# The tiles of x start at 64 modulo 256 bytes in place of 0

## The chip, the cores and the metric

The kernel runs on one core of a Trainium2 chip. The metric is the device time of one execution in microseconds. PE is TensorE (PEld its weight loads), DVE is VectorE, ACT is ScalarE, POOL is GpSimd, SP is SyncE, which here only starts DMAs.

## The reference

A windowed attention (768 positions, 8 heads of 64, a batch of 4) is followed by a feed-forward layer with a rational activation. Cut to what matters:

```python
scores = scale * np.matmul(q, k.transpose(0, 1, 3, 2))
scores = np.where(keep, scores + bias, -1e9)        # a local window of 96 and 8 global keys
a = softmax(scores)
x = np.matmul(a, v)                                 # -> (3072 tokens, 512)
h = x @ w_in                                        # (512, 2048)
P = a[0] + a[1] * h + a[2] * h**2 + a[3] * h**3
Q = 1.0 + np.abs(b[0]) * np.abs(h) + np.abs(b[1]) * h**2
out = (P / (Q + 1e-06)) @ w_out                     # (2048, 512)
```

## The kernel before

The 3072 tokens are worked in 12 chunks of 256. Each chunk has 8 attention units (a pair of heads for 128 tokens each) and 8 feed-forward units f (256 of the 2048 columns of w_in each). A program of tokens (LEAD), a loop over t with priorities (PRI) and a last list (TAIL) set the order of the instructions on every engine; PE and SP follow the order of the code.

The products of the feed-forward layer keep float32's precision with three float32r matmuls each: a high and a low part of one operand against a high and a low part of the other (high by high, low by high, high by low). For chunk 0 alone x stays one float32 tile, x0, and line 332 multiplies it in float32; the names below are those of chunks 1 to 11.

- `st_x` (line 737) takes the attention's output of a chunk out of PSUM. ACT writes the high part into the tile xh (line 753), DVE the low part, xl (line 763, in `st_xl`). Each is 128 partitions by 4 x 256 numbers, 4096 bytes of a partition. There are two buffers of each, used in turn by the chunks.
- `st_ffn1` (line 322) computes h = x @ w_in for one unit in two halves y. Line 340 issues 12 matmuls for each half: 4 tiles of 128 rows, and for each the products high weight by xh, high weight by xl, low weight by xh. The **stationary** operand, which a LDWEIGHTS loads, is a block of 128 x 128 of the weights; the **moving** operand is 256 columns of xh or xl. A unit is 24 such matmuls in a row.
- The activation runs on ACT, DVE and POOL and leaves g, high and low.
- `st_ffn2` (line 426) multiplies by w_out: line 442 issues 12 matmuls for a unit. Here g is stationary and 512 columns of w_out (high or low) move. `st_last2` (line 445) does the same for the last unit, and there, at the end, on half the columns: line 451 has matmuls of 256 moving columns too.

Where tiles stand: pools are laid one behind the other in a partition, each tile behind the one made first before it. A small tile `gap` of 24 numbers (line 218) stands at the end of the constants, so that all that follows starts at 64 modulo 256. Start addresses in the built program, in bytes of a partition:

| tile | start | modulo 256 | used by |
|---|---|---|---|
| win_h, high weights of w_in | 2368 | 64 | line 340, stationary |
| wout_h, high weights of w_out | 18752 | 64 | lines 442 and 451, moving |
| h tiles, the rest of the high weights | 52544 and on, each 4096 | 64 | lines 340 (stationary), 442 (moving) |
| w..l, low weights | 85312 and on, each 2048 | 64 | lines 340 (stationary), 442 (moving) |
| pad0 | 183616 | 64 | nobody |
| xh, two buffers | 183808, 187904 | 0 | line 340, moving |
| xl, two buffers | 192000, 196096 | 0 | line 340, moving |
| pad1 | 200192 | 0 | nobody |
| sp, the six buffers of the activation, g | 200256 and on | 64 | g: lines 442 and 451, stationary |

The blocks that a matmul takes out of these tiles lie at multiples of 512 bytes from their start, so the remainder modulo 256 is the same for each of them. Line 340 thus has its moving operand at 0 and its stationary one at 64; lines 442 and 451 have both at 64.

The two pads are tiles that `pad` (line 494) makes and POOL sets to zero, when chunk 1's first tiles of x are made (line 743 ff.).

Of the kernel before, what the change touches and what calls it, by code (L numbers as in the profile page):

```python
# [9 lines left out]
F32 = mybir.dt.float32  # L10
# [7 lines left out]
P = 128  # L18
# [124 lines left out]
def tile_kernel(ctx: ExitStack, tc: tile.TileContext, q, k, v, n_global, n_local,  # L143
                w_in, w_out, ca, cb, out):
    nc = tc.nc
# [16 lines left out]
    pl = SimpleNamespace(tmps=TMPS, gbufs=GBUFS, split=False)  # L162
# [5 lines left out]
    def unit(u):  # L168
        c, j = divmod(u, UPC)
        t, p = divmod(j, NPAIR)  # L170
        b, i = divmod(2 * c + t, NT)
        return c, t, p, b, i
# [51 lines left out]
    def staged(dt, shape, name):  # L224
        return stage.tile([P, *shape], dt, tag="s", name=name, bufs=8)
# [265 lines left out]
    pTs = {}  # L491
    ops = {}

    def pad(pool, n, name):
        nc.gpsimd.memset(pool.tile([P, n], F32, tag=name, name=name, bufs=1), 0.0)

    def blocks_of(x, i):
        return x if i else x[..., 0, :]

# [209 lines left out]
    def run_of(u):  # L709
        return 4 if u >= PAIRS else 2  # L710
# [26 lines left out]
    def st_x(u0):  # L737
        n, m = run_of(u0), u0 // 2
        c, t, p, b, i = unit(u0)
        if c not in xT and c == 0:  # L740
            xT[c] = staged(F32, (NCT, TOK), "x0")
        elif c not in xT:
            if c == 1:
                pad(pl.att, 48, "pad0")
            xT[c] = (pl.att.tile([P, NCT, TOK], FR, tag="xh", name=f"xh{c}"),
                     pl.att.tile([P, NCT, TOK], FR, tag="xl", name=f"xl{c}"))
            if c == 1:
                pad(pl.att, 16, "pad1")
        cs = slice(t * P, (t + 1) * P)
        if c == 0:  # L750
            nc.scalar.copy(out=xT[c][:, p:p + n, cs], in_=ops.pop(m))
            return
        nc.scalar.copy(out=xT[c][0][:, p:p + n, cs], in_=ops[m])
# [13 lines left out]
    def windowed():  # L767
# [4 lines left out]
        for x in range(2):  # L772
# [14 lines left out]
        parts = dict(L=lambda u: st_load(u, True), V=load_v, sp=st_split, sr=st_gather, qT=st_qkT, qE=st_qkE, kG=st_kG,  # L787
                     s=st_score, kg=st_kg, t=st_max, x=st_soft, r=st_total, n=st_norm, T=st_pT, tw=st_spread, P=st_pTE, zw=st_scatter, vp=load_vp, o=st_pv,
                     vg=st_vg, y=st_x, z=st_xl, W=w_load, a=w_scale, b=w_floor, c=w_sign, d=w_bits, h=w_high, l=w_low,
                     f1=st_ffn1, e1=st_ew1, e2=st_poly, eq=st_sum, e3=st_ew3, e4=st_ew4, gh=st_high, gl=st_low, f2=st_ffn2,  # L790
                     BL=st_blocks, BZ=st_zero, H=st_hold, O=st_out, D=st_send, F=st_last2)
# [289 lines left out]
```

## Time and profile before

| | |
|---|---|
| median of 3 runs | 695.6 us (694.66 to 695.7) |
| profiled execution | 694.39 us, its span 692.6 us |
| PE busy | 666.9 us, 96% of the span |
| DVE, ACT, POOL busy | 536.0, 531.6, 365.4 us |
| line 340 | 2112 matmuls, 31% of the chain that ended last |
| line 442 | 1032 matmuls, 31% of that chain |

The profile lists each instruction with its start and how long it took. Matmuls overlap, and their ends are modelled: a matmul of line 340 is listed with some 280 ns, though the next one starts some 115 ns later. What one costs is therefore read from start to start, or from the chain of work that ended last, which lists matmuls that follow each other as one piece with its length. "PEclk" is the share of TensorE's clock that was granted, 1.00 being 2.4 GHz.

### The profile page before, as it was taken

To read this page: it belongs to the slowest core of one execution; us is meant where nothing else is said; L and a number is where in the kernel's file an instruction comes from. 1 tells how busy PE (TensorE), PEld (TensorE's weight loads), DVE (VectorE), ACT (ScalarE), POOL (GpSimd) and SP (SyncE) were. 2 spreads that over 40 slices of the span, in tenths; PEclk is the share of its full clock that TensorE was granted. 3 is DMA by queue.
4 is the path that set the end of the run, shared out by engine and by line. 5 is a ranking of instruction groups with operands and counts; after the bars stand their busy time and mean duration, and the time that the engine had idled before them with its cause. 6 is when DMAs were issued, how large, how long until landed. Compare 5 with 4: busy or idle time off the path is not lost.

```text
span 692.6 us, 17121 instructions
## 1 busy us (share of the span) xinstructions
PE 666.9 (96%) x6167; PEld 572.6 (83%) x6167; DVE 536.0 (77%) x1319; ACT 531.6 (77%) x1174; POOL 365.4 (53%) x487
## 2 busy tenths in 40 slices
PE   5799999999999999999999999999999999999995
PEld 4577768768788898888889889888889889898994
DVE  5899999897987777777787777777777777765664
ACT  6899999876677877777786876876887876866773
POOL 2475545676446456456556546545555545543441
PEclk9999999999999999999999999999999999999998
DMA  7874646413576757655557657655457555320001
GB/s 189 272 207 101 208 119 188 121 46 87 146 183 164 184 127 179 158 138 142 139 132 183 167 129 180 166 127 152 132 139 188 151 150 150 101 85 1 31 2 36
DMA packets 161215, 95.22 MB, mean 137 GB/s; under 512 B 100064, under 2 KB 141152, under 8 KB 161120
## 3 DMA queue, kind: packets, MB, share of 16 engines
q1 hardware_dynamic: 161120, 94.02, 52.0%
q8 instruction: 51, 0.84, 0.6%
q14 instruction: 44, 0.36, 0.2%
HBM read 66.39 MB, written 27.59 MB: 136 GB/s over the span
## 4 chain that ended last, share of the span: by engine, by line
PE 74%; ACT 11%; DVE 7%; DMA 2%; issue 2%; POOL 1%; SPq 1%; DVEq 0%; POOLq 0%; ACTq 0%
PE h L340 31%; PE acc L442 31%; PE o L724 5%; PE s L601 4%; ACT pr L645 2%; ACT r L271 1%; PE acc L438 1%; DMA r<-in_moe_w_in_dram 1%; ACT qzero L564 1%; DVE fu L404 1%; DVE q L403 1%; PE h L332 1%; DVE fu L402 1%; ACT fs L397 1%; DVE pr L636 1%
## 5 line engine op out<-in xcount | busy, mean ns | idle before, releaser
L386 POOL TENSOR_TENSOR fa<-fa,fs 128x512 f32<-128x512 f32 (+1 forms) x86 | 110.0, 1279 | 144.2 <-ACT fs L374 143.9
L397 ACT ACTIVATE fs<-fa,coef 128x512 f32<-128x512 f32 (+1 forms) x97 | 69.8, 720 | 87.1 <-POOL fa L386 84.6
L658 POOL TENSOR_SCALAR pr<-pr,stats 128x160 f32<-128x160 f32 (+2 forms) x170 | 68.3, 421 | 128.2 <-DVE stats L652 87.0
L402 DVE SCALAR_TENSOR_TENSOR fu<-fu,coef,q 128x512 f32<-128x512 f32 (+1 forms) x97 | 71.6, 738 | 62.2 <-ACT q L398 61.8
L442 PE MATMUL acc<-wout_h,g 128*128 128x512 f32 x352 | 117.1, 393 | 2.0 <-POOL g L415 2.0
L415 POOL TENSOR_TENSOR g<-fu,g 128x512 fp32r<-128x512 f32 x84 | 108.1, 1287 | 10.1 <-ACT g L412 5.9
L442 PE MATMUL acc<-h,g 128*128 128x512 f32 x336 | 110.8, 391 | 0.1
L340 PE MATMUL h<-xh,win_h 128*128 128x256 f32 x352 | 101.3, 288 | 0.2 <-DVE fu L382 0.2
L340 PE MATMUL h<-xh,h 128*128 128x256 f32 x352 | 101.0, 287 | 0.0
L340 PE MATMUL h<-xl,win_h 128*128 128x256 f32 x352 | 98.3, 279 | 0.5 <-DVE xl L763 0.5
L340 PE MATMUL h<-xl,h 128*128 128x256 f32 x352 | 98.2, 279 | 0.0
L645 ACT ACTIVATE pr<-pr,stats 128x160 f32<-128x160 f32 (+2 forms) x192 | 82.5, 433 | 10.9 <-DVE stats L636 10.9
L372 ACT ACTIVATE fu<-h,coef 128x512 f32<-128x512 f32 x94 | 73.0, 776 | 22.9 <-PE h L340 21.8
L381 DVE TENSOR_TENSOR fu<-fu,h 128x512 f32<-128x512 f32 (+1 forms) x97 | 65.6, 677 | 31.0 <-ACT fs L374 29.6
L442 PEld LDWEIGHTS acc<-wout_h,g 128*128 128x128 f32 x352 | 65.9, 188 | 15.0 <-POOL g L415 2.8
L442 PEld LDWEIGHTS acc<-h,g 128*128 128x128 f32 x336 | 63.0, 188 | 12.5 <-POOL g L415 0.6
L382 DVE SCALAR_TENSOR_TENSOR fu<-fu,coef,h 128x512 f32<-128x512 f32 (+1 forms) x97 | 71.2, 734 | 2.7
L403 DVE SCALAR_TENSOR_TENSOR q<-fa,coef,q 128x512 f32<-128x512 f32 (+1 forms) x97 | 72.1, 743 | 0.0
L340 PEld LDWEIGHTS h<-xh,win_h 128*128 128x128 f32 x352 | 66.1, 188 | 4.4 <-issue 1.8
L340 PEld LDWEIGHTS h<-xh,h 128*128 128x128 f32 x352 | 66.1, 188 | 4.3 <-issue 2.8
L340 PEld LDWEIGHTS h<-xl,win_h 128*128 128x128 f32 x352 | 66.2, 188 | 2.1 <-DVE xl L763 0.7
L404 DVE SCALAR_TENSOR_TENSOR fu<-q,fu 128x512 f32<-128x512 f32 (+1 forms) x97 | 66.2, 682 | 2.1
(262 smaller groups left out, 1676.3 us busy)
## 6 DMA issues: line engine op xcount, KB each, us to landing
pT<-z SPq DMA_DIRECT2D x30, 512.0 KB, 4.0
z<-T SPq DMA_DIRECT2D x120, 80.0 KB, 2.3
zq<-sp SPq DMA_DIRECT2D x144, 64.0 KB, 1.8
qk<-zq SPq DMA_DIRECT2D x36, 256.0 KB, 2.8
r<-in_moe_w_in_dram SPq DMA_DIRECT2D x16, 512.0 KB, 5.1
r<-in_moe_w_out_dram SPq DMA_DIRECT2D x16, 512.0 KB, 4.0
nat<-in_q_dram SPq DMA_DIRECT2D x48, 128.0 KB, 4.2
nat<-in_k_dram SPq DMA_DIRECT2D x48, 128.0 KB, 4.0
```

The costliest lines, as they stand in the source:

```text
L340: nc.tensor.matmul(out=h_of(f, y), lhsT=w[:, fs], rhs=x[:, ct, :], start=(n == 0), stop=(n == 3 * NCT - 1))
L372: nc.scalar.activation(out=u, in_=h, func=AF.Identity, scale=a3, bias=a2)
L382: nc.vector.scalar_tensor_tensor(out=u, in0=u, scalar=a1, in1=h, op0=ALU.add, op1=ALU.mult)
L386: pace(side(f, SUM_V).tensor_tensor(out=a, in0=a, in1=s, op=ALU.add))
L397: nc.scalar.activation(out=s, in_=a, func=AF.Ln, bias=q1)
L402: nc.vector.scalar_tensor_tensor(out=u, in0=u, scalar=a0, in1=r, op0=ALU.add, op1=ALU.mult)
L403: nc.vector.scalar_tensor_tensor(out=r, in0=a, scalar=q1, in1=r, op0=ALU.add, op1=ALU.mult)
L404: nc.vector.scalar_tensor_tensor(out=u, in0=r, scalar=2.0, in1=u, op0=ALU.subtract, op1=ALU.mult, reverse0=True)
L415: pace(side(f, G_V, f == NU - 1 and ys == 1).tensor_tensor(out=gs[f][:, 1, ys], in0=ew[f]["u"][:, ys], in1=gs[f][:, 0, ys], op=ALU.subtract))
L442: nc.tensor.matmul(out=acc, lhsT=gs[f][:, z, y, ts], rhs=w, start=(start and n == 0), stop=(stop and n == 2))
L645: nc.scalar.activation(out=d, in_=d, func=AF.Exp, scale=-1.0, bias=st[:, x:x + 1], accum_out=st[:, 2 + 2 * x:3 + 2 * x])
L658: (nc.vector if u < NORMS else nc.gpsimd).tensor_scalar(out=d, in0=d, scalar1=st[:, 6 + x:7 + x], scalar2=0.0, op0=ALU.mult, op1=ALU.add)
```

## The change

The helper `pad` and its two calls go. Nothing else in the code is changed.

```diff
-    def pad(pool, n, name):
-        nc.gpsimd.memset(pool.tile([P, n], F32, tag=name, name=name, bufs=1), 0.0)
-
...
         elif c not in xT:
-            if c == 1:
-                pad(pl.att, 48, "pad0")
             xT[c] = (pl.att.tile([P, NCT, TOK], FR, tag="xh", name=f"xh{c}"),
                      pl.att.tile([P, NCT, TOK], FR, tag="xl", name=f"xl{c}"))
-            if c == 1:
-                pad(pl.att, 16, "pad1")
```

The pads were 192 and 64 bytes. Without them the built program has the buffers of xh at 183616 and 187712 and those of xl at 191808 and 195904, all 64 modulo 256. All tiles behind them stand 256 bytes lower, so their remainder is what it was; all tiles ahead of them stay. Line 340 then has both operands at 64 modulo 256, as lines 442 and 451 had before.

On PE, DVE, ACT and SP the same instructions stand in the same order. On POOL two are gone. There, before, in the attention of the first chunks (k and kG are keys, pr the probabilities of a unit, r and w parts of the weights):

```order
L658 TENSOR_SCALAR pr_701<-pr_701,stats 128x256 x2
L611 COPY k_174<-kG_65 128x8
L495 MEMSET pad_775 128x48
L495 MEMSET pad_779 128x16
L658 TENSOR_SCALAR pr_735<-pr_735,stats 128x256 x2
L273 TENSOR_SCALAR r_7_753<-r_7_753 128x512
L290 TENSOR_TENSOR w_0_0l<-w_0_0f,win_h 128x512
```

And after, at the same place on POOL (line numbers are 3 lower there, since the lines of `pad` are gone):

```order
L655 TENSOR_SCALAR pr_701<-pr_701,stats 128x256 x2
L608 COPY k_174<-kG_65 128x8
L655 TENSOR_SCALAR pr_735<-pr_735,stats 128x256 x2
L273 TENSOR_SCALAR r_7_753<-r_7_753 128x512
L290 TENSOR_TENSOR w_0_0l<-w_0_0f,win_h 128x512
```

The two MEMSETs left the row, and nothing took their place.

## Rows read from the trace of the kernel before

**Rows 1.** The page: PE's busy time, and the chain's shares by engine.
```profile
PE 666.9 (96%) x6167; PEld 572.6 (83%) x6167; DVE 536.0 (77%) x1319; ACT 531.6 (77%) x1174; POOL 365.4 (53%) x487
...
PE 74%; ACT 11%; DVE 7%; DMA 2%; issue 2%; POOL 1%; SPq 1%; DVEq 0%; POOLq 0%; ACTq 0%
```

**Rows 2.** Stretches: length, busy us of PE, PEld, DVE, ACT, POOL, PEclk, DMA.
```profile
60.00:200.00 140.00, 135.83 (x968) 105.22 (x966) 127.37 (x287) 118.05 (x265) 80.61 (x102) 1.00 0.45 126
200.00:400.00 200.00, 199.64 (x2189) 176.99 (x2190) 152.75 (x383) 152.47 (x329) 110.57 (x141) 1.00 0.63 157
400.00:600.00 200.00, 200.00 (x2132) 178.23 (x2131) 151.04 (x377) 151.51 (x324) 110.75 (x142) 1.00 0.59 148
```

**Rows 3.** The chain by time, 605 to 628 us: start us, length us, what.
```profile
605.45 2.92 PE h L340 x24
608.37 2.73 PE acc L442 x12
611.10 2.83 PE h L340 x24
613.93 2.72 PE acc L442 x12
616.65 2.83 PE h L340 x24
...
627.74 1.90 PE o L724 x32
```

**Rows 4.** Timeline of PE, a unit of line 340 behind attention: start us, us, what.
```profile
346.66 0.38 PE L340 MATMUL h<-xh,win_h 128*128 128x256 f32 x1
346.88 0.28 PE L340 MATMUL h<-xl,win_h 128*128 128x256 f32 x1
347.00 0.28 PE L340 MATMUL h<-xh,w_1l 128*128 128x256 f32 x1
...
349.38 0.28 PE L340 MATMUL h<-xh,w_1l 128*128 128x256 f32 x1
349.49 0.39 PE L442 MATMUL acc<-wout_h,g 128*128 128x512 f32 x1
349.72 0.40 PE L442 MATMUL acc<-w_2l,g 128*128 128x512 f32 x1
349.95 0.62 PE L442 MATMUL acc<-wout_h,g 128*128 128x512 f32 x2
350.41 0.39 PE L442 MATMUL acc<-w_3l,g 128*128 128x512 f32 x1
```

**Rows 5.** Timeline of PE, the next unit of line 340, behind line 442.
```profile
352.00 0.39 PE L442 MATMUL acc<-wout_h,g 128*128 128x512 f32 x1
352.22 0.28 PE L340 MATMUL h<-xh,h 128*128 128x256 f32 x1
352.34 0.28 PE L340 MATMUL h<-xl,h 128*128 128x256 f32 x1
...
355.05 0.39 PE L442 MATMUL acc<-wout_h,g 128*128 128x512 f32 x1
```

**Rows 6.** Line 340 from 346.95 to 349.35 us: count, ns min/median/max, first and last start.
```profile
L340 PE MATMUL h<-xl,win_h x8: 276/276/276, 346.9 to 349.3; 128*128 128x256 f32 x8
L340 PEld LDWEIGHTS h<-xh,w_1l x8: 187/188/188, 346.9 to 349.3; 128*128 128x128 f32 x8
```

**Rows 7.** The same of line 340 from 352.25 to 354.90 us.
```profile
L340 PE MATMUL h<-xl,h x8: 281/281/281, 352.3 to 354.8; 128*128 128x256 f32 x8
L340 PEld LDWEIGHTS h<-xh,w_2l x8: 192/192/192, 352.3 to 354.8; 128*128 128x128 f32 x8
```

**Rows 8.** Those two stretches, columns as in rows 2.
```profile
346.90:349.30 2.40, 2.40 (x23) 2.40 (x23) 2.40 (x12) 2.22 (x9) 0.67 (x1) 1.00 0.35 87
352.30:354.90 2.60, 2.60 (x24) 2.60 (x23) 1.52 (x3) 1.14 (x2) 2.60 (x3) 1.00 1.23 285
```

**Rows 9.** Timeline of PE at the end, line 451 with 256 moving columns.
```profile
684.28 0.28 PE L451 MATMUL acc<-h,g 128*128 128x256 f32 x1
684.39 0.28 PE L451 MATMUL acc<-w_15l,g 128*128 128x256 f32 x1
684.51 0.28 PE L451 MATMUL acc<-h,g 128*128 128x256 f32 x1
685.31 0.39 PE L451 MATMUL acc<-h,g 128*128 128x256 f32 x1 [0.52 <-DVE o L471]
685.53 0.28 PE L451 MATMUL acc<-w_15l,g 128*128 128x256 f32 x1
685.65 0.28 PE L451 MATMUL acc<-h,g 128*128 128x256 f32 x1
```

**Rows 10.** Timeline of POOL at the pads: start us, us, what, [idle before, releaser].
```profile
55.09 0.18 POOL L495 MEMSET pad<- 128x48 f32 x2
61.04 1.36 POOL L658 TENSOR_SCALAR pr<-pr,stats 128x256 f32<-128x256 f32 x2 [5.76 <-DVE stats L652]
```

**Rows 11.** The writers of xh and xl (as in rows 6), and a cast to a tile at 64 (as a group: busy us, mean ns).
```profile
L753 ACT CAST xh<-o x26: 373/565/582, 58.3 to 629.7; 128x512 fp32r<-128x512 f32 x18, 128x256 fp32r<-128x256 f32 x8
L763 DVE TENSOR_TENSOR xl<-o,xh x26: 404/670/683, 62.0 to 631.1; 128x512 fp32r<-128x512 f32 x18, 128x256 fp32r<-128x256 f32 x8
L286 ACT CAST win_h<-w_1f 128x512 fp32r<-128x512 f32 x4 | 2.5, 633 | 0.0
```

## The prediction

> **What bounds the kernel now.** I read the page first: PE is busy for 96% of the span and holds 74% of the chain that ended last [rows 1]. Then the busy times by stretch: from 200 to 600 us PE is busy for all but 0.4 of 400 us, while from 60 to 200 us it stands idle for 4.2 of 140 [rows 2]. Then the chain in order of time, which from about 200 us on runs through PE and repeats one pattern [rows 3]. A stretch of attention matmuls comes first, then a unit of line 340 (24 matmuls), a unit of line 442 (12), a unit of line 340, a unit of line 442. PE sets the end there, so a nanosecond more on each matmul of line 340 is a nanosecond on the time; before 200 us PE waits now and then, and its gains or losses are partly hidden.
>
> The same 24 matmuls do not always cost the same. A unit behind attention takes 2.92 us in the chain, one behind line 442 takes 2.83 us [rows 3], and the first of these includes the start after attention. In the timeline the step from start to start shows it plainly. Behind attention the first step is 0.22 us, and then 23 steps go from 346.88 to 349.49: 2.61 / 23 = 113.5 ns, the **short step** [rows 4]. Behind line 442, 24 steps go from 352.22 to 355.05: 2.83 / 24 = 117.9 ns, the **long step** [rows 5]. The listed durations say the same, 276 ns in the one and 281 ns in the other, and in the long unit the load of the low weights is listed with 192 ns, in the short one with 188 [rows 6, 7]. Clock and company do not explain it: the granted clock is 1.00 (2.4 GHz) in both, and DVE and ACT are busier beside the short unit, POOL and DMA beside the long one [rows 8]. The shape, operands and remainders are the same too. What differs is what PE did just before. So line 340 has two steady ways to run, 4.4 ns apart, and falls into one of them by how it starts. From 100 us on the chain has 42 pieces of 24 at 2.83 us, and 32 behind attention at 2.92 to 3.00 us; [rows 3] has the pattern.
>
> Line 442 has a second way as well: directly behind a short unit its first two steps go from 349.49 to 349.95, 0.23 us each, before it settles near 2.72 / 12 = 227 ns; behind a long unit it takes 2.72 us in place of 2.73 [rows 3, 4]. Its 227 ns are twice 113.4 ns for twice the columns, so it runs the short way with both operands at 64.
>
> **The change part by part.** *The two MEMSETs.* They take 0.18 us on POOL at 55.09, and POOL then stands idle for 5.76 us until DVE's statistics come [rows 10]. Nobody waits for a pad. That is worth nothing; without that cover it would be 0.18 us.
>
> *The writers of xh and xl.* ACT and DVE write the same shapes to another remainder, 26 times each with a median of 565 and 670 ns [rows 11]. The nearest row that writes float32r to a tile at 64 is the cast of line 286, 633 ns from another source [rows 11]; if the 70 ns were due to the remainder, ACT would get 26 x 0.07 = 1.8 us more of work over 690 us, and a gain of that size is as thinkable. ACT is not what the chain waits for after 200 us. I take 0.
>
> *Line 340.* This is the whole question: 11 chunks x 8 units x 24 = 2112 matmuls whose moving operand goes from 0 to 64 modulo 256, while the weights that are loaded beside it stay at 64. The trace has no row of line 340 in that state, and the only matmuls of this width and type with both operands at 64 are the six of line 451 at the end. Behind line 442, whose steps were short, they run 684.28, 684.39, 684.51: one step of 0.11 and one of 0.12. After the pause: 685.31, 685.53, 685.65: the first step of 0.22, as after attention, and then 0.12 [rows 9]. So of three steps that are not first ones two are long and one is short, and the first step after a pause is the one that line 340 has too. Bounds: if every unit ran short, the 42 long units would shrink from 2.83 to 24 x 113.5 = 2.72 us, 42 x 0.11 = 4.6 us less, and the 32 units of line 442 behind a short one would lose their 0.01 us at the start, 0.3 us: **-4.9 us**. If every unit ran long, the 32 units behind attention would gain 22 steps x 4.4 ns = 0.097 us each, 3.1 us, and the line 442 behind them would give the 0.3 us back: **+2.8 us**. If each step were the 0.12 us of the dearest row of line 451, the 42 units would cost 24 x 0.120 = 2.88, 0.05 more each (2.1 us), and the 32 would gain 22 x 6.5 ns = 0.14 (4.6 us), minus 0.3: +6.4 us.
>
> I take the second, all units long, because that is what two of the three steps in [rows 9] are, and because the one after a pause is long there, where line 340 with its operand at 0 has its short ones. The sum is 0 + 0 + 2.8 us. Against the profiled execution (692.6 us of span, 694.39 us in all) that is 697.2 us; that run is 1.2 us under the median, so against the median of 695.6 us I get **698.4 us**.
>
> **The rivals.** *All units short: faster.* Line 442, at 64 and 64, settles in its short way within a few steps and keeps it [rows 3, 4]. With line 340 at 0 and 64 the two lines may each be at home in a way that does not suit the other: after a short unit of one, the other starts long [rows 4, 5]. With the same remainders in both, line 340 could simply go on in line 442's short way. It would give 695.6 - 4.9 = 690.7 us. Against it stand the steps of 0.12 us behind line 442 in [rows 9], which should be 0.113. It decides if the step behind line 442 stays short beyond the first matmul.
>
> *No change.* The two ways may hang on when a weight load starts beside a running matmul, and not on the addresses. Then the same units stay short and long, and the time is 695.6 us. For it: the same unit with the same remainders runs both ways [rows 4, 5]. Against it: the first step behind line 442 is short in [rows 9] and long in [rows 5]. The Trainium skill, page "TensorE: Matmul & The Clock Gate", section "Step-by-step: what each phase is for", says that PE has two independent read ports to SBUF and that loading the next weights takes no read bandwidth from the running matmul; by that rule addresses would play no part and this rival would hold. The trace agrees only in part: a load of one shape is listed with 188 and with 192 ns [rows 6, 7].
>
> *Dearer than long: slower by more.* This is the 0.12 us of one row of line 451 for all units, 695.6 + 6.4 = 702.0 us, the forecast's sign with another price.
>
> *The pads do nothing to the addresses.* That is excluded: the addresses in the built program did move.
>
> **How the numbers follow.** All long, or between that and no change, 0.34; dearer than long, 0.14; no change, 0.22; short everywhere or in part, 0.30. A measurement of this kernel can tell about 0.2%, 1.4 us, from no change. Slower by over that: 0.34 + 0.14 = 0.48. Within it: 0.22. Faster: 0.30. Cases of both signs hold most of the chance, so the range goes from a little beyond all short, 690.3 us, to a little beyond the dearest row, 703.0 us; I leave 0.1 out on either side for a way to run that no row shows. The forecast's own range is 696.9 to 700.0 us.
>
> **What would show it.** In the profile after, the chain's pieces of 24 of line 340 tell it at once: 2.83 us behind line 442 and about 3.02 behind attention, with 281 ns as the listed duration of nearly all, if the forecast holds; 2.72 and 2.92 with 276 ns if the faster rival does; the mixture of before if nothing changed; 2.88 and more if it is dearer. Line 442's units should be 2.72 us nearly everywhere in the first case. POOL should show nothing at 55 us, and the writers of xh and xl their 565 and 670 ns. What would make the prediction wrong is that line 451, six matmuls with other operands and another output, is no measure of line 340, or that the way a unit starts behind attention shifts with the operand.

## The result, and the profile after

The changed kernel takes 703.1 us (median of 6 runs, 701.92 to 705.97) against 695.65 us of the kernel before in 6 runs: a ratio of 1.0113, 95% interval 1.0087 to 1.0139. It is slower by 1.1%, about 7.5 us. (The ratio is not the quotient of the two medians, which would be 1.0107.) Ratios, here and below, leave out runs in a slow state, of which there was one, of 836.64 us at a granted clock of 0.755, among the ten of the kernel under "All lower by 64". The forecast was 698.4 us; the direction was right, the size was not: 7.5 us in place of 2.8. The time lies 0.1 us beyond the range's upper end of 703.0, which is less than its own runs differ by.

The page of the changed kernel, its busy times and its chain by engine:

```profile
span 700.1 us, 17119 instructions
...
PE 675.1 (96%) x6167; PEld 579.8 (83%) x6167; DVE 536.0 (77%) x1319; ACT 532.4 (76%) x1174; POOL 365.2 (52%) x485
...
PE 82%; ACT 10%; DVE 3%; SPq 1%; DMA 1%; issue 1%; POOL 1%; DVEq 0%; POOLq 0%; ACTq 0%
```

The span is 7.5 us longer than the 692.6 us of before, and PE is busy for 8.2 us more than in [rows 1], with the same 6167 matmuls. POOL has lost its two instructions; the other engines do what they did. The chain in order of time, in the stretch that answers to [rows 3]:

```profile
605.92 2.75 PE acc L442 x12
608.67 0.79 PE s L598 x28
609.46 1.96 PE o L721 x32
611.41 3.07 PE h L340 x24
614.48 2.75 PE acc L442 x12
617.23 2.87 PE h L340 x24
620.10 2.75 PE acc L442 x12
```

Each kind of piece of lines 340 and 442 is dearer: 24 matmuls of line 340 behind attention take 3.07 us in place of 2.92, behind line 442 2.87 in place of 2.83, and 12 of line 442 2.75 in place of 2.72 or 2.73 [rows 3]. The timeline of PE shows the steps of a unit behind line 442, the place of [rows 5]:

```profile
353.52 0.39 PE L442 MATMUL acc<-wout_h,g 128*128 128x512 f32 x1
353.75 0.28 PE L340 MATMUL h<-xh,h 128*128 128x256 f32 x1
353.86 0.28 PE L340 MATMUL h<-xl,h 128*128 128x256 f32 x1
353.98 0.28 PE L340 MATMUL h<-xh,w_2l 128*128 128x256 f32 x1
...
356.62 0.40 PE L442 MATMUL acc<-wout_h,g 128*128 128x512 f32 x1
356.85 0.40 PE L442 MATMUL acc<-w_4l,g 128*128 128x512 f32 x1
357.09 0.62 PE L442 MATMUL acc<-wout_h,g 128*128 128x512 f32 x2
```

The first step is 0.11 us. Then 23 steps go from 353.86 to 356.62: 2.76 / 23 = 120.0 ns. This third way to run is what nearly all of line 340's matmuls follow now, and the two of before, 113.5 and 117.9 ns, are gone. Behind it line 442 starts with steps of 0.23 and 0.24 us. In the kernel before, behind the unit of [rows 5], it goes on from 355.05 in steps of 227 ns at once:

```profile
355.28 0.39 PE L442 MATMUL acc<-w_4l,g 128*128 128x512 f32 x1
355.50 0.62 PE L442 MATMUL acc<-wout_h,g 128*128 128x512 f32 x2
```

Durations of line 340 (count, ns min/median/max, first and last start), the load of the high weights in the unit of [rows 5]:

```profile
L340 PEld LDWEIGHTS h<-xl,h x8: 187/188/188, 352.2 to 354.7; 128*128 128x128 f32 x8
```

And in the unit of the changed kernel that is shown above:

```profile
L340 PEld LDWEIGHTS h<-xl,h x8: 188/192/192, 353.8 to 356.3; 128*128 128x128 f32 x8
L340 PE MATMUL h<-xl,h x8: 283/283/283, 353.9 to 356.4; 128*128 128x256 f32 x8
```

283 ns stands where it was 276 or 281 [rows 6, 7], and the load of the high weights, 187 or 188 ns in the unit of before, has a median of 192.

The pieces of the chain from 100 us on add up as follows. 42 units of line 340 behind line 442 went from 2.83 to 2.87 us: 1.7 us. 32 behind attention went from 2.92 to 2.94 (18 of them) and 2.99 to 3.00 (14) to 3.06 to 3.07 and 3.13: 0.14 us each, 4.5 us. 72 units of line 442 went from 2.72 or 2.73 to 2.75 us: some 0.026 each, 1.9 us. That is 8.1 us, against 7.5 us of span. The traces say where the difference lies: PE's 1201st matmul, at 196 us, still starts 0.6 us earlier in the changed kernel, and the last one starts 7.1 us later, so that from there on the loss is 7.7 us. What the changed kernel was ahead by in the first 200 us is a matter of two single executions, and no run shows its cause.

### The profile page after: what moved, and what is told of

It reads as the page before. It is cut to its first block, busy times and chain, and to the rows that moved or that the text cites. A ratio compares the mean times of both kernels' runs of the same rounds, so it can differ in the third digit from the quotient of the medians.

```text
span 700.1 us, 17119 instructions
## 1 busy us (share of the span) xinstructions
PE 675.1 (96%) x6167; PEld 579.8 (83%) x6167; DVE 536.0 (77%) x1319; ACT 532.4 (76%) x1174; POOL 365.2 (52%) x485
## 4 chain that ended last, share of the span: by engine, by line
PE 82%; ACT 10%; DVE 3%; SPq 1%; DMA 1%; issue 1%; POOL 1%; DVEq 0%; POOLq 0%; ACTq 0%
PE h L340 33%; PE acc L442 32%; PE o L721 5%; PE s L598 4%; PE h L332 3%; PE acc L438 2%; ACT pr L642 2%; PE s L584 1%; DMA r<-in_moe_w_in_dram 1%; ACT qzero L561 1%; ACT r L271 1%; ACT fu L372 1%; PE tp L667 1%; ACT fs L397 1%; ACT q L398 1%
## 5 line engine op out<-in xcount | busy, mean ns | idle before, releaser
L340 PEld LDWEIGHTS h<-xl,h 128*128 128x128 f32 x352 | 67.4, 191 | 1.4 <-issue 0.5
```

Source lines behind the costliest of these rows:

```text
L340: nc.tensor.matmul(out=h_of(f, y), lhsT=w[:, fs], rhs=x[:, ct, :], start=(n == 0), stop=(n == 3 * NCT - 1))
```

## The experiments

**Theory A**, formed on this result: what counts is the distance, modulo 256 bytes, between the start of the moving operand and the start of the weights that are loaded beside it. In the kernel before it is 0 - 64, that is 192; in the changed one it is 0. **Rival B**: x's own remainder counts. **Rival C**: the MEMSETs count, or the 256 bytes by which the tiles behind x moved. All kernels below ran beside the kernel before on the same chip, and ratios are to it.

### The pads stay, and x moves

The second pad goes ahead of x as well, so that only x moves, by 64 bytes (xh from 183808 to 183872). This is 256 bytes above its place in the changed kernel, with the same remainder.

```diff
             if c == 1:
                 pad(pl.att, 48, "pad0")
+                pad(pl.att, 16, "pad1")
...
-            if c == 1:
-                pad(pl.att, 16, "pad1")
```

> Both pads and both MEMSETs stay, but they stand together ahead of the tiles of x (256 bytes in all), so that x starts at 64 modulo 256 as in the changed kernel, and every other tile stands where it did before. Theory A (what counts is the distance modulo 256 between the start of the moving operand and that of the weights loaded beside it: at distance 0 a matmul of line 340 steps 120 ns): 120 ns steps everywhere, units of 2.87 us behind line 442, about 703 us. Rival C (the MEMSETs, or the 256 bytes by which the tiles behind x moved, make the difference): steps of 113.4 and 117.8 ns as before, about 695.6 us.

Measured: 703.56 us against 694.6, 1.0127 (1.0095 to 1.0159). The chain has the pieces of the changed kernel:

```profile
612.57 3.07 PE h L340 x24
615.64 2.75 PE acc L442 x12
618.39 2.87 PE h L340 x24
```

Rival C falls: with both MEMSETs there and every other tile at home, 64 bytes under x make the whole difference. And 256 bytes more under x, against the changed kernel, make none.

### All at 0

The changed kernel, with one tile of 192 bytes ahead of win_h: weights, w_out, g and x all start at 0 modulo 256.

```diff
+    nc.gpsimd.memset(const.tile([P, 48], F32, name="lead"), 0.0)
     win_h = const.tile([P, NCT, HALF * TOK], FR, name="win_h")
```

> The changed kernel with one tile of 192 bytes ahead of win_h: now the weights, g and x all start at 0 modulo 256. Theory A (distance of the two operands): distance is 0 as in the changed kernel, so 120 ns steps everywhere and about 703 us. Rival B (the moving operand's own start counts, 0 good and 64 bad): 113.4 and 117.8 ns as before, about 695.6 us.

Measured: 705.63 us against 694.6, 1.0136 (1.0100 to 1.0172), with the same pieces again:

```profile
615.47 3.07 PE h L341 x24
618.54 2.75 PE acc L443 x12
621.29 2.87 PE h L341 x24
```

x stands at 0, as in the kernel before, and takes the changed kernel's time. Rival B falls.

### All lower by 64, distances as before

The same added tile of 192 bytes in the kernel before, pads kept. Modulo 256 every tile is then lower by 64: x is at 192, the weights and g at 0.

> The kernel before with one tile of 192 bytes ahead of win_h, pads kept: weights, w_out and g start at 0 modulo 256 and x at 192, so every pair of operands has the distance that it has in the kernel before, and none of those tiles its remainder. Theory A (only distances count, those at the borders between lines too): steps, units and first steps as in the kernel before, 113.4 ns behind attention, 117.8 behind line 442, 2.72 and 2.73 us in line 442, about 694.6 us. Rival B (a remainder of its own counts beside the distance): another mixture, as x at 192 gave before (702 us) or as with the weights at 128 (698.5 us).

Measured: 694.58 us against 694.65, 0.9995 (0.9982 to 1.0008). The chain is that of [rows 3], piece by piece:

```profile
605.16 2.92 PE h L341 x24
608.08 2.73 PE acc L443 x12
610.81 2.83 PE h L341 x24
613.64 2.72 PE acc L443 x12
616.36 2.83 PE h L341 x24
```

No tile of x, weights or g has the remainder that it had, every pair has its distance, and the time is the same to within 0.2%. This is the clearest run for theory A.

### The stationary operand alone

The changed kernel, x left at 64; line 340 takes its blocks of weights 64 bytes further on (in the last block of each 512 columns, 192 bytes further back). They are the wrong columns, so this kernel's output is not the reference's; the work is the same.

```diff
+        ws = fw + 16 if fw < 3 * P else fw - 48
+        ws = slice(ws, ws + P)
...
-                nc.tensor.matmul(out=h_of(f, y), lhsT=w[:, fs], rhs=x[:, ct, :],
+                nc.tensor.matmul(out=h_of(f, y), lhsT=w[:, ws], rhs=x[:, ct, :],
```

> The changed kernel, x at 64 modulo 256, but line 340 takes its blocks of weights 16 columns further on (48 columns back for the last block of each 512), so that every stationary operand starts at 128 modulo 256. The output is then not x times w_in: the columns of w_in are the wrong ones, and nothing else is left out. Only the stationary operand's remainder differs from the changed kernel. Theory A (distance of moving minus stationary, now 192 as in the kernel before): steps of 113.4 and 117.8 ns in the same units as before, about 695.6 us. Rival B (x's own start counts): 120 ns steps and about 703 us.

Measured: 698.55 us against 694.8, 1.0059 (1.0037 to 1.0081).

```profile
608.14 2.94 PE h L342 x24
611.07 2.74 PE acc L444 x12
613.82 2.83 PE h L342 x24
616.65 2.75 PE acc L444 x12
```

The 2.87 us behind line 442 are back at 2.83, and units behind attention's last products (line 724) at 2.94, 2.92 before, by moving the weights alone. But the time stops half way: where a unit follows the scores directly it takes 3.08 us (13 units; 2.99 before), and line 442 keeps its 2.75 us. At the borders between lines the distances are not those of before: the last x, which is xh, moves beside the load of the first g at distance 0 here, and at 192 before. In the run above, where the borders are those of before too, nothing is left over.

For line 442 the traces settle it. In the four kernels whose xh is at distance 0 from g, this one among them, the first five steps of line 442 take some 233, 236, 228, 232 and 231 ns behind every kind of unit, before it settles at 227; here it does so behind units at 113.4 and at 117.8 ns. In the three whose xh is at 192 from g it does not: nearly all their units of line 442 take 2.72 or 2.73 us, in the last experiment even behind units of 3.06 us. So the dear start goes with the pair at the border, and not with a step of 120 ns ahead of it. What makes the units behind the scores long here (14 of 16, none of them before) was not tried by itself.

### Line 442 at the same distance

The kernel before, with 64 bytes ahead of g: line 442, too, has its operands at distance 192, like line 340. **Theory D**, tried here: the units of line 340 behind line 442 are long in the kernel before because line 442 runs at another distance, 0, and would be short behind a line 442 at 192.

```diff
         if f not in gs:
+            if not pl.split and "g" not in paced:
+                paced["g"] = True
+                pad(pl.ffn, 16, "padg")
```

> The kernel before with 64 bytes ahead of g: line 442's stationary operand starts at 128 and its moving one at 64, distance 192, the same as line 340 has there; line 340 is untouched. Theory D (the long way of line 340 behind line 442 comes from the two lines having different distances): both lines go on in each other's short way, units of line 340 behind line 442 take 2.72 us and line 442 behind them 2.72, about 690.7 us. Rival (the long way comes from the change of the width of 512 to 256 columns, whatever the distance): 2.83 us still, and 695 us or, if the new distance costs line 442 anything, more.

Measured: 700.86 us against 694.8, 1.0082 (1.0065 to 1.0099).

```profile
602.67 2.83 PE h L340 x24
605.50 2.80 PE acc L445 x12
608.30 0.79 PE s L604 x29
...
613.96 2.79 PE acc L445 x12
616.75 2.83 PE h L340 x24
619.59 2.80 PE acc L445 x12
622.38 2.74 PE h L340 x24
```

Theory D falls in the main: of 43 units of line 340 behind line 442, five are short, 2.74 us, the others keep 2.83. The rival that its expectation names, the change of width, is not settled by this. And line 442 pays: 2.79 to 2.80 us for each unit in place of 2.72 or 2.73. With 512 moving columns, of the two distances tried, 192 is the bad one and 0 the good one, the reverse of line 340 with 256.

### The other remainders of x

The two pads were split differently, in six kernels, always with 256 bytes in all, so that nothing but x moves. The edit for x at 128:

```diff
-                pad(pl.att, 48, "pad0")
+                pad(pl.att, 16, "pad0")
...
-                pad(pl.att, 16, "pad1")
+                pad(pl.att, 48, "pad1")
```

> The kernel before with the pads split 16 and 48 numbers: x starts at 128 modulo 256, 64 above the weights; all else stands where it did. Theory A says only that it is not the 120 ns of distance 0: a mixture of 113 to 118 ns, 690 to 699 us. If nearness of the two operands in either direction costs alike, the same mixture as at 0 (64 below): 695.6 us. Rival B (0 is good, all else bad): 120 ns, about 703 us.

> The kernel before with the pads split 32 and 32 numbers: x starts at 192 modulo 256, 128 above and 128 below the weights; all else stands where it did. Theory A: not 120 ns; if a larger distance is better, short steps of 113.4 ns in all units and about 691 us. Rival B (0 is good, all else bad): 120 ns, about 703 us.

> The kernel before with the pads split 56 and 8 numbers: x at 32 modulo 256, distance 224. If the cost goes with the distance in a smooth way, it lies between 120 ns (distance 0) and the mixture of 113.4 and 117.8 (distance 192), some 118 ns and 699 us. If only whole 64-byte pieces count, it is either as before (695.6 us) or as after (703 us).

> The kernel before with the pads split 8 and 56 numbers: x at 96 modulo 256, distance 32. Smooth: between 120 ns (distance 0) and the mixture at distance 64 (mean 117.0 ns, 699 us), some 118.5 ns and 701 us. Whole 64-byte pieces: as after (703 us) or as with x at 128 (699 us).

> The kernel before with the pads split 40 and 24 numbers: x at 224 modulo 256, distance 160. Between the mean of 119.2 ns at distance 128 and 116.0 at distance 192 if the cost is smooth in the distance: some 117.6 ns and 699 us. If short steps have a window of their own around 192, units at 113.4 ns alone and about 691 us.

> The kernel before with the pads split 24 and 40 numbers: x at 160 modulo 256, distance 96. Between 117.0 ns at distance 64 and 119.2 at distance 128 if smooth: some 118 ns and 700 us. Nothing in the runs so far makes it faster than the kernel before.

Measured, with the two kernels of the change in their places. Unit lengths are those of most pieces of the chain; of the two behind attention the first is for units behind line 724, the second for those behind the scores. The mean is taken over line 340's steps from start to start of at most 125 ns; this leaves out some 70 longer ones at x = 160, so that row's mean is a little low:

| x modulo 256 | distance | mean step, ns | line 340 behind line 442, us | behind attention, us | ratio to before |
|---|---|---|---|---|---|
| 0 (before) | 192 | 116.0 | 2.83 | 2.92, 2.99 | 1 |
| 32 | 224 | 118.3 | 2.84 | 3.03, 3.09 | 1.0100 (1.0074 to 1.0127) |
| 64 (after) | 0 | 119.7 | 2.87 | 3.07, 3.13 | 1.0113 (1.0087 to 1.0139) |
| 96 | 32 | 117.0 | 2.80 | 3.03, 3.06 | 1.0049 (1.0029 to 1.0068) |
| 128 | 64 | 117.0 | 2.83 | 3.02, 2.98 | 1.0053 (1.0034 to 1.0073) |
| 160 | 96 | 119.7 | 2.88 | 3.07, 3.13 | 1.0117 (1.0097 to 1.0138) |
| 192 | 128 | 119.2 | 2.88 | 3.04, 3.10 | 1.0104 (1.0076 to 1.0132) |
| 224 | 160 | 118.4 | 2.85 | 3.02, 3.08 | 1.0062 (1.0041 to 1.0083) |

All seven other remainders are slower than x at 0. The cost is not smooth in the distance, which four of the expectations had as one case: 0 and 96 are the dearest, 32 and 64 between them are the cheapest after 192. Pieces of 64 bytes do not settle it either, as 32 and 0 differ, and 96 and 64. Only x at 0 has all units behind attention settle at 113.4 ns, 34 in the trace (the chain above holds 32). With x at 128, distance 64, 16 of them do, 14 of these behind the scores; at the other distances none does. At most of those there is no steady step at all, but a pattern that repeats: with x at 160, steps from 115 to 125 ns behind attention. At x = 96 the units behind line 442 are the cheapest of all, but those behind attention are not:

```profile
607.89 3.03 PE h L340 x24
610.92 2.73 PE acc L442 x12
613.65 2.80 PE h L340 x24
616.46 2.75 PE acc L442 x12
```

### xl alone

pad1 stands between xh and xl: xh at 0 (distance 192), xl at 64 (distance 0).

```diff
-            xT[c] = (pl.att.tile([P, NCT, TOK], FR, tag="xh", name=f"xh{c}"),
-                     pl.att.tile([P, NCT, TOK], FR, tag="xl", name=f"xl{c}"))
+            xh = pl.att.tile([P, NCT, TOK], FR, tag="xh", name=f"xh{c}")
             if c == 1:
                 pad(pl.att, 16, "pad1")
+            xT[c] = (xh, pl.att.tile([P, NCT, TOK], FR, tag="xl", name=f"xl{c}"))
```

> The kernel before with pad1 moved between xh and xl: xh stays at 0 modulo 256, xl starts at 64, all else stands where it did. One matmul in three then has its moving operand at distance 0 from the weights, two at distance 192. If each matmul pays by its own pair: one step of 120 ns in three beside two of 113.4 or 117.8, a mean of some 117.3 ns and about 698.5 us. If the pairs act on each other through the start that one leaves to the next, the pattern is a new one and the mean is not the weighted one; a single pair at distance 0 could then bring all steps near 120 ns, about 703 us.

Measured: 699.02 us against 694.18, 1.0067 (1.0048 to 1.0086).

```profile
608.92 3.06 PE h L340 x24
611.99 2.73 PE acc L442 x12
614.72 2.83 PE h L340 x24
617.55 2.72 PE acc L442 x12
```

The mean step is 118.1 ns, not the weighted 117.3. The units behind line 442 keep the length of the kernel before, 2.83 us, those behind line 724 come to within 0.01 us of the changed kernel's 3.07, and those behind the scores take 3.08 in place of its 3.13. So the matmuls do not each pay for their own pair: with one pair in three at distance 0 the short way is lost altogether. Line 442 keeps its 2.72 and 2.73 us, since xh, the last to move ahead of it, stands where it did.

No kernel of the twelve is faster than the one before, and none pointed to a version that would be.

## Why the prediction was right or wrong

**What bounds the kernel: right.** PE sets the end, its chain went from 74% to 82% in the changed kernel, and the pieces of that chain carry the difference.

**The MEMSETs and the writers of x: right.** POOL's next instruction still waits for DVE, 5.88 us now, and xh and xl are written in 564 and 669 ns, as against 565 and 670 [rows 10, 11]. POOL, where the MEMSETs stood:

```profile
53.68 0.19 POOL L608 COPY k<-kG 128x8 f32<-128x8 f32 x1
59.75 1.37 POOL L655 TENSOR_SCALAR pr<-pr,stats 128x256 f32<-128x256 f32 x2 [5.88 <-DVE stats L649]
```

**The ways to run: right in kind.** That line 340 falls into a steady step, and that the way hangs on the two operands' addresses, was the frame of the forecast and holds for the kernels before and after. The step that it fell into is one that no row of line 340 had shown. The rival of no change is refuted by the run in which only x moves.

**The price of a step: wrong, and this is the step that failed.** Of three bounds I took "every unit long", 117.9 ns and +2.8 us, over the dearest row, 120 ns and +6.4 us, to which I gave 0.14. The rows of line 451 were the right ones to read: with both operands at 64 and 256 columns they are the changed line 340 in small, and they show its first two steps behind line 442, 0.11 and then 0.12 [rows 9]. I counted them as samples, "two of three are long", and took the known long step for them. A timeline with hundredths of a microsecond cannot tell 117.9 from 120. And the first step, 0.11 us, is no sample of the steady way: in the changed kernel nearly every unit behind line 442 starts with it once and then runs at 120.0 ns. The term "every unit long" put 0 on the units behind line 442 and 3.1 us on those behind attention; they cost 1.7 and 4.5.

**The size of the terms.** For the dearest row the sum was 2.1 us for the units behind line 442, 4.6 for those behind attention, and -0.3 for line 442. Measured were 1.7, 4.5 and +1.9. So even that sum was short, by its third term, which had the wrong sign: I took line 442 to start well behind any unit that is not short, because it does so behind the long ones of before [rows 3]. The step of the unit ahead is not what sets it: with the stationary operand alone moved, line 442 starts dear behind units at 113.4 and 117.8 ns too. I overlooked that the change also moves the last xh from distance 192 to 0 from the first g. That third term is 2.2 us off; with the first two as measured, 6.2 us, the time would be 701.8 us, inside the range.

**The faster rival: refuted, twice.** It had line 340 go on in line 442's short way once the remainders agree. They agree in the changed kernel and it does so for one step. Given the same distance of 192 instead, line 442 itself got dearer, and 38 of 43 units of line 340 behind it stayed long.

**The page's rule.** The Trainium skill, page "TensorE: Matmul & The Clock Gate", section "Step-by-step: what each phase is for", has the weight load and the running matmul read SBUF through two independent ports, so that the load takes no read bandwidth from the matmul. These runs do not agree for float32r, where addresses should then play no part: the step went from 120.0 ns to 117.8 and 113.4 by moving the stationary operand alone, and the eight kernels of the table, which differ in where x starts, have mean steps from 116.0 to 119.7 ns. The Trainium skill, page "SBUF — State Buffer", section "Door 1: The DMA port swizzle", gives SBUF 16-byte lines and a penalty for each access that crosses to a new one. That does not explain it either, since all the starts tried are multiples of 32 bytes.

**Open.** That the distance of the two operands decides, within line 340 and at the border to line 442, is shown. That it counts modulo 256 bytes rests on one pair of kernels, whose x stands 256 bytes apart at the same cost (1.0113 and 1.0127, with intervals that overlap); modulo 128 would not do, since distances 64 and 192 differ. Why it does, what in SBUF or TensorE the two reads share, and why 192 suits 256 columns and 0 suits 512, no run here shows. Nor was it tried whether finer distances than 32 bytes matter.

## What to carry to other kernels

Where TensorE is the bound with float32r matmuls, each with its own weight load, the start addresses of the two operands against each other are worth about 1% here: try the eight distances of 32 bytes modulo 256 with a pad, and for each width of matmul by itself, since the good one for 512 columns was a bad one for 256. Count the pair at the border too, the last operand that moves and the first weights of the next line. Move every tile of a pair together, or keep the distances, when a pool or a constant is added: 192 bytes at the front cost nothing when all distances stayed. And read a step from a run of equal matmuls, in nanoseconds, past its first ones: three steps in hundredths of a microsecond hid both the price and the way.

## What the runs showed of the hardware

- The step of a float32r matmul of 256 moving columns with its own weight load hangs on the distance of its operands modulo 256 bytes: steady at 113.4 or 117.8 ns at 192 and at 120.0 ns at 0, and at 96, for one, a pattern of 115 to 125 ns, at the same granted clock (1.00 in the stretches from 200 to 600 us of the kernels at 192, 0 and 96).
- At one distance there can be two steady values, and the start decides: units of the same shape ran at 113.5 ns behind attention and at 117.9 ns behind line 442 [rows 4, 5].
- Adding 192 bytes to all operands alike changes nothing: 0.9995 (0.9982 to 1.0008).
- A matmul of 512 columns went the other way: some 227 ns at distance 0, and 2.79 / 12 = 233 ns at distance 192.
- The pair at the border between two lines counts too: line 442 took 2.75 us, with first steps of 233, 236, 228, 232 and 231 ns, where the last xh ahead of it was at distance 0 from the first g, and 2.72 or 2.73 us where it was at 192.
